# Dilated attention in blocks of one parity: seventeen blocks for eighteen, and transposes two blocks at a time

## The chip, the core and the metric

The kernel runs on one core of one Trainium2 chip. A core has five engines with queues of their own: TensorE (PE) multiplies matrices, VectorE (DVE), ScalarE (ACT) and GpSimd (POOL) work on elements, and SyncE (SP) here issues transfers (DMA). SBUF is the working memory with 128 partitions; PSUM, in eight banks, takes TensorE's results. A product has 128 columns of weights, loaded first, and a moving operand of up to 512 columns. The metric is the time of one execution on the device in microseconds, and less is better.

## The reference

A layer of 2048 tokens with 448 features, in bf16: attention, then a gated mixer, both behind a layernorm and with a residual sum.

```python
def _A_ref(x, wqkv, wo):            # H = 16 heads of Dh = 28
    W, dil = (8, 2)
    qkv = ...x @ wqkv...
    off = jnp.arange(W) * dil
    idx = pos[:, None] - off[None, :]
    mask = idx >= 0
    ...
    logits = jnp.einsum('bhsd,bhswd->bhsw', q, kg) * scale
    attn = _softmax(jnp.where(mask, logits, -1e9), axis=-1)
    o = jnp.einsum('bhsw,bhswd->bhsd', attn, vg)
    return ...o... @ wo

def _B_ref(x, w_in, w_sp, b_sp, w_out):
    z = _gelu(x @ w_in)                      # 448 -> 1792
    z1, z2 = z[..., :896], _layernorm(z[..., 896:])
    g = einsum('ts,bsf->btf', w_sp, z2) + b_sp
    return (z1 * g) @ w_out

h  = x + _A_ref(_layernorm(x), A_wqkv, A_wo)
h2 = h + _B_ref(_layernorm(h), B_w_in, B_w_sp, B_b_sp, B_w_out)
```

A token attends to itself and to the tokens 2, 4, ..., 14 before it, so an even token sees even tokens alone, and an odd one odd tokens alone.

## The kernel before

**Order of work.** The kernel is written as 963 jobs. A job is a few instructions for one engine, with the buffers it reads and writes (`Res`), PSUM banks that it takes or frees (`Ticket`), and an estimate of its time. A planner (`Planner.order`, L273) sorts them in the build: it places one job after another on its engine, by rank from the list `PRIO` among those ready within `LOOK[engine]`, with fixed costs for switching between forms of products (`SWITCH`). What comes out is a fixed order for each engine, and each instruction waits for semaphores of those it depends on. `ON` (L68) puts single jobs on another engine than their usual one.

**Stages.** Tokens lie in 16 tiles of 128. The input tiles get their layernorm (`ln_stats`, `ln_rstd` on POOL, `ln_norm` L682), are transposed to `xhT` (features by tokens; four tiles by TensorE, twelve by DMA), and are projected to queries and keys (`qk`, evacuated by `qe` into `qkT`, [128, 8, 2048], in the order of tokens) in six pieces of tokens (`QT`, L81).

**Attention blocks.** `GEOM` (L17) lists 18 blocks as (first token, queries, keys before it): one of 128 queries, nine of 112 with 16 keys before them, eight of 114 with 14. For each block b:
- `v` (L778): values of the block's 128 keys, two blocks in one job: `xhT` as weights, `wv` moving, evacuated by `ve` into `V1`
- `lg` (L853): 16 products of 28 rows, keys by queries, one for each head, in two jobs; `ex` (L861) exponentiates them from PSUM into `E`, 8 heads at a time
- `mk` (L867): one multiplication by `maskb`, which holds ones on the eight diagonals with a step of two
- `o` (L876): 16 products, `E` as weights, `V1` moving with a column of ones for the sum; `rc` and `om` (L884, L887) normalize into `otm`; `od` copies the last 64 features once more behind the 448, so that after the transpose they lie in both halves of the partitions
- `oT` (L896 to L903): a DMA transpose to `OT` (features by tokens). Where the block's first token isn't a multiple of 16, it goes to a buffer `OTs`, and `oc` copies it on.

As soon as 256 tokens are complete, `project` (L805) multiplies them with `wo` (`y`), adds the residual (`h`, L820), normalizes (`n1`), and transposes each tile by DMA to `hnT` (`hT`, L829).

**Mixer.** `z2` (L912) and `z1` (L960) multiply `hnT` with `w_in`. Eleven of the 16 z2 tiles (`RAW2`) are moved out raw and get their gelu later; the other gelus wait for the last exponential, as ACT loads another table for them. From L1005 on come 28 groups of 16 products with the spatial weights (`wsp_la`, `wsp_lb`, `wsp_hi`, loaded by transposing DMAs), the gate (L1023, L1026), and the output product (L1038).

All DMAs are issued by SP in one queue. A product over 448 features is three products of 128 rows and one of 64; in pairs, the two half-height ones use the upper and lower half of the array at the same time (`product`, L552).

Of the kernel before, what the change touches and what calls it, by code (L numbers as in the profile page):

```python
# [5 lines left out]
S_TOK = 2048  # L6
D = 448
# [7 lines left out]
NAB = 18  # L15
OTR = 1024
GEOM = [(0, 128, 0)] + [(128 + 112 * i, 112, 16) for i in range(9)] + [(1136 + 114 * i, 114, 14) for i in range(8)]  # L17
# [7 lines left out]
LOOK = {'pe': 0.009410205530073946, 'act': 1e-09, 'dve': 0.19498114580727732, 'pool': 1e-09, 'sp': 0.13408016923274957}  # L25
PRIO = [0, 2, 3, 4, 1, 5, 9, 10, 8, 6, 7, 11, 13, 14, 12, 22, 23, 38, 39, 34, 44, 47, 49, 0, 0, 19, 16, 12, 9, 13, 29,
# [36 lines left out]
KEY = dict(x=-10.145, xs=0.685, qk=-3.702, qkg=-1.064, v=-1.761, ve=-6.148, qe=-3.15, lg=-1.488, ex=5.497,  # L63
           mk=-3.215, o=2.696, om=0.603, oT=-1.054, hh=0.0, y=-5.759, h=0.564, ln2=4.478, hT=19.942, z2=74.834,
           z2s=0.028, zr=2.556, zrs=0.21, z1=34.42, z1s=2.041, g=84.462, gs=0.172, wo=1.509, wl=-9.273,
           wls=4.361, wp=-9.955)
WINB = 2
ON = {'xe0_1': 'act', 'nd0_10': 'dve', 'nd0_12': 'dve', 'nd0_13': 'dve', 'nd0_14': 'dve', 'nd0_15': 'dve', 'wp0_1':  # L68
      'act', 'wp1_1': 'act', 'wp2_0': 'act', 'wp2_1': 'act', 'wp3_1': 'act', 'qe4_1': 'dve', 'qe4_3': 'dve', 'nd1_0': 'dve',
      'od3': 'dve', 'od4': 'dve', 'nd1_3': 'dve', 've8': 'dve', 'od9': 'dve', 'nd1_8': 'dve', 'oc12': 'act', 'nd1_10': 'dve',  # L70
      'od14': 'dve', 'oc15': 'act', 'nd1_13': 'dve', 'nd1_14': 'dve', 'nd1_15': 'dve', 'z2c2': 'dve', 'z2c4': 'dve', 'z2c7':
# [1039 lines left out]
```

## Time and profile before

| what | value |
|---|---|
| median of 3 runs | 243.84 us (242.87 to 244.76) |
| the profiled execution | 242.9 us, span of its profile 241.2 us |
| granted TensorE clock | 1.00 |
| DMA | 23.23 MB in 66,468 packets, 46.1% of 16 engines' span in the queue for loads and transposes |
| first spatial product (L1014) | starts at 111.1 us |
| last logit product, last weighted sum | start at 79.3 and 98.0 us |
| transposes issued by SP | 12 to xhT, 11 to OT, 7 to OTs, 16 to hnT, 32 of spatial weights |

The profile page gives each engine's busy time, the span in 40 slices, and the chain of work that ended last. Rows of groups name a line, an engine and an operation, out<-in tiles, shapes, and how often (x): total busy time and the mean of one. Matrix products overlap, so the duration of one (354 ns for 448 columns) is longer than the distance from one to the next; the distance is read from the chain or the timeline. "L565" is the line of a helper that issues all products over 448 features, and "L576" that of a helper for copies, so tile names tell them apart. DVE and ACT in slices of 6 us, in tenths of busy time:

| engine | page, 40 slices |
|---|---|
| DVE | 4799778989989999999761344024044724410754 |
| ACT | 2899868777885899555030000000000000302100 |
| POOL | 7335300233454212431401000000000000000000 |

### The profile page before, as it was taken

To read this page: it belongs to the slowest core of one execution; us is meant where nothing else is said; L and a number is where in the kernel's file an instruction comes from. 1 tells how busy PE (TensorE), PEld (TensorE's weight loads), DVE (VectorE), ACT (ScalarE), POOL (GpSimd) and SP (SyncE) were. 2 spreads that over 40 slices of the span, in tenths; PEclk is the share of its full clock that TensorE was granted. 3 is DMA by queue.
4 is the path that set the end of the run, shared out by engine and by line. 5 is a ranking of instruction groups with operands and counts; after the bars stand their busy time and mean duration, and the time that the engine had idled before them with its cause. 6 is when DMAs were issued, how large, how long until landed. Compare 5 with 4: busy or idle time off the path is not lost.

```text
span 241.2 us, 4323 instructions
## 1 busy us (share of the span) xinstructions
PE 234.0 (97%) x1736; PEld 114.3 (47%) x1758; DVE 152.7 (63%) x330; ACT 93.6 (39%) x118; POOL 42.4 (18%) x93
## 2 busy tenths in 40 slices
PE   7899999999999999999999999999999999999995
PEld 5665445454545444544444444444444544444443
DVE  4799778989989999999761344024044724410754
ACT  2899868777885899555030000000000000302100
POOL 7335300233454212431401000000000000000000
PEclk9999999999999999999999999999999999999999
DMA  6936475975955957967599960000000111000012
GB/s 188 347 98 91 100 148 108 161 214 106 96 117 97 154 102 161 111 136 215 109 188 168 193 127 3 0 0 0 0 3 1 57 38 41 19 0 0 19 60 76
DMA packets 66468, 23.23 MB, mean 96 GB/s; under 512 B 58896, under 2 KB 66192, under 8 KB 66448
## 3 DMA queue, kind: packets, MB, share of 16 engines
q1 hardware_dynamic: 66448, 22.95, 46.1%
q8 instruction: 14, 0.23, 0.4%
q14 instruction: 6, 0.05, 0.1%
HBM read 6.83 MB, written 1.84 MB: 36 GB/s over the span
## 4 chain that ended last, share of the span: by engine, by line
PE 80%; DVE 10%; POOL 3%; DMA 2%; issue 1%; SPq 1%; ACT 1%; DVEq 0%
PE psum L1014 40%; PE psum L565 27%; PE psum L1038 9%; DVE E L867 3%; DMA x_tm<-in_A_x_dram 2%; PE psum L876 2%; DVE st L677 2%; DVE xn L688 2%; POOL rs L672 2%; PE psum L852 2%; SPq L591 1%; DVE otm L887 1%; POOL rs L671 1%; DVE x_tm L820 1%; ACT E L861 1%
## 5 line engine op out<-in xcount | busy, mean ns | idle before, releaser
L1014 PE MATMUL psum<-wsp_hi,z2p 128*128 128x512 bf16 x217 | 50.9, 379 | 0.5 <-issue 0.2
L981 ACT ACTIVATE z1p<-psum 128x1024 bf16<-128x1024 f32 x14 | 14.1, 1024 | 94.3 <-PE psum L565 94.3
L1023 DVE TENSOR_TENSOR ub<-psum,bb 128x512 bf16<-128x512 f32 x28 | 19.4, 692 | 45.3 <-PE psum L1014 44.8
L861 ACT ACTIVATE E<-psum 128x896 bf16<-128x896 f32 (+2 forms) x36 | 31.7, 929 | 8.4 <-PE psum L852 8.4
L1014 PEld LDWEIGHTS psum<-wsp_hi,z2p 128*128 128x128 bf16 x224 | 21.8, 98 | 26.4 <-issue 0.4
L565 PE MATMUL psum<-xhT,wqk 128*128 128x512 bf16 (+5 forms) x185 | 27.8, 306 | 1.6 <-DVE wqk L576 0.8
L1014 PE MATMUL psum<-wsp_lb,z2p 128*128 128x512 bf16 x111 | 26.3, 379 | 0.1
L1014 PE MATMUL psum<-wsp_la,z2p 128*128 128x512 bf16 x109 | 25.7, 379 | 0.2
L565 PE MATMUL psum<-w_in,hnT 128*128 128x448 bf16 (+1 forms) x128 | 25.0, 353 | 0.0
L565 PE MATMUL psum<-hnT,w_in 128*128 128x512 bf16 (+1 forms) x108 | 23.4, 379 | 0.3 <-issue 0.2
L1038 PE MATMUL psum<-w_out,z1p 128*128 128x448 bf16 (+1 forms) x119 | 22.5, 341 | 0.0
L867 DVE TENSOR_TENSOR E<-E,maskb 128x1792 bf16<-128x1792 bf16 (+2 forms) x18 | 19.5, 1098 | 1.1 <-ACT E L861 1.0
L940 DVE BATCH_NORM_STATS2 st<-z2p 128x6 f32<-128x448 bf16 x32 | 18.9, 610 | 1.9 <-ACT z2p L936 1.7
L677 DVE BATCH_NORM_STATS2 st<-x_tm 128x6 f32<-128x448 bf16 x32 | 19.1, 612 | 1.3 <-DMA x_tm<-in_A_x_dram 0.9
L1026 DVE TENSOR_TENSOR z1p<-ub,z1p 128x512 bf16<-128x512 bf16 x28 | 11.8, 424 | 12.4 <-ACT z1p L981 11.6
L565 PEld LDWEIGHTS psum<-xhT,wqk 128*128 128x128 bf16 (+1 forms) x192 | 12.9, 97 | 12.4 <-issue 2.9
L672 POOL TENSOR_TENSOR rs<-rs,negh 128x2 f32<-128x2 f32 (+2 forms) x22 | 17.8, 810 | 1.8
L1045 DVE TENSOR_TENSOR srg<-psum,x_tm 128x448 bf16<-128x448 f32 (+1 forms) x17 | 10.0, 595 | 11.4 <-PE psum L1038 11.2
L1014 PEld LDWEIGHTS psum<-wsp_lb,z2p 128*128 128x128 bf16 x112 | 10.9, 98 | 13.2 <-issue 0.2
L1014 PEld LDWEIGHTS psum<-wsp_la,z2p 128*128 128x128 bf16 x112 | 10.9, 98 | 13.1 <-issue 0.2
L1038 PEld LDWEIGHTS psum<-w_out,z1p 128*128 128x128 bf16 x119 | 11.6, 98 | 10.2
L576 ACT ACTIVATE qkT<-psum 128x1024 bf16<-128x1024 f32 (+2 forms) x22 | 15.4, 716 | 2.5 <-PE psum L565 1.9
(57 smaller groups left out, 229.1 us busy)
## 6 DMA issues: line engine op xcount, KB each, us to landing
w_in<-in_B_w_in_dram SPq DMA_DIRECT2D x8, 224.0 KB, 3.4
out_dram<-srg SPq DMA_DIRECT2D x16, 112.0 KB, 1.7
x_tm<-in_A_x_dram SPq DMA_DIRECT2D x3, 448.0 KB, 6.7
w_out<-in_B_w_out_dram SPq DMA_DIRECT2D x1, 784.0 KB, 6.7
wraw<-in_A_wqkv_dram SPq DMA_DIRECT2D x1, 672.0 KB, 5.7
bb<-in_B_b_sp_dram SPq DMA_DIRECT2D x1, 512.0 KB, 4.7
wv<-in_A_wqkv_dram SPq DMA_DIRECT2D x1, 336.0 KB, 6.7
wo<-in_A_wo_dram SPq DMA_DIRECT2D x1, 336.0 KB, 6.1
```

The costliest lines, as they stand in the source:

```text
L565: ins = e.matmul(o, w, x, start=g not in seen, stop=left[g] == 0, **kw)
L576: j = pl.job(name, eng, key, [(lambda e: e.activation(o(), i(), AF.Copy) if eng == "act" else e.tensor_copy(o(), i()), list(reads), list(w ...
L672: (lambda e: e.tensor_tensor(R, A, negh[:, 0:1].to_broadcast([128, n]), ALU.pow), [rr, r_negh], r_rs[k][m:m + n])],
L677: [(lambda e: e.bn_stats(st[:, m, :], src), [rsrc], [r_st[k][m]])], dve_t(D))
L861: return e.activation(o, i, AF.Exp, scale=SCALE)
L867: return e.tensor_tensor(a, a, maskb[:, 0:1, pad:pad + nq].to_broadcast([NK, NHEAD, nq]), ALU.mult)
L940: [(lambda e, m=m, k=k: e.bn_stats(st3[:, m, k, :], z2p[:, m, D * k:D * (k + 1)]), [r_z2[m]], [r_st[2][m]])], dve_t(D))
L981: return e.activation(o, i, AF.Gelu_apprx_tanh)
L1014: ins = e.matmul(psv(tk), z2p[:, s, 128 * fc:128 * fc + 128], w[:, 512 * (tc % 2):512 * (tc % 2) + 512], start=(s == 0), stop=(s == NB - 1))
L1023: [(lambda e, tc=tc, s=s, tk=tk: e.tensor_tensor(ub[:, s, :], psv(tk), bb[:, 512 * tc:512 * tc + 512], ALU.add), [r_bb], [r_ub[s]])], dve_ ...
L1026: [(lambda e, fc=fc, tc=tc, s=s: e.tensor_tensor(z1p[:, fc, 512 * tc:512 * tc + 512], ub[:, s, :], z1p[:, fc, 512 * tc:512 * tc + 512], AL ...
L1038: ins = e.matmul(psv(tk, 0, c1 - c0), z1p[:, fc, 128 * m:128 * m + 128], w_out[:, fc, c0:c1], start=(fc == 0), stop=(fc == FC7 - 1))
```

## The change

Blocks are now of one parity. `GEOM` holds (first token, queries, keys before it, step): blocks 0 and 1 take the 128 even and the 128 odd tokens of the first 256; then seven pairs take 240 tokens each, 120 queries with 8 keys before them; the last block, 112 queries with 16 keys before it, has step one again. That makes 17. In a block of one parity the mask is a band of eight diagonals in a row, so `maskb` has two masks, one for either kind.

What follows from it:
- `qkT` holds even tokens first, then odd ones, 1024 apart; `qe` writes them apart as it leaves PSUM. For the last block, the last 128 tokens are also copied to `qkL` in order.
- `values` reads every second token of `xhT` as weights.
- Two blocks of a pair lie side by side in `otm` (four slots, before three) and are transposed in one DMA to `OTs`, then `oc` copies both into every second column of `OT`, in two pieces where the ring of 1024 tokens wraps. Eight such copies, on ACT by default; `ON` puts five of them on POOL. The last block is transposed straight to `OT`.
- The second layernorm's tiles are transposed two at a time; `hnT` is now [128, tile, 4, 128], and the reads of `z2` and `z1` follow.
- `bb` (the spatial bias) moves to the place of the attention buffers, and `pads` clears more columns of `E`.
- `PRIO`, `LOOK` and `ON` are new; `KEY`, `RAW2`, `WLH`, `QT` and the stages' code behind attention are the same but for the layout.

```diff
-NAB = 18
+NAB = 17
-GEOM = [(0, 128, 0)] + [(128 + 112 * i, 112, 16) for i in range(9)] + [(1136 + 114 * i, 114, 14) for i in range(8)]
+GEOM = [(r, 128, 0, 2) for r in range(2)] + [(256 + 240 * i + r, 120, 8, 2) for i in range(7) for r in range(2)] + [(1936, 112, 16, 1)]
-LOOK = {'pe': 0.009410205530073946, 'act': 1e-09, 'dve': 0.19498114580727732, 'pool': 1e-09, 'sp': 0.13408016923274957}
...
+LOOK = {'pe': 1e-09, 'act': 0.13510754282655793, 'dve': 0.16074023548447497, 'pool': 0.11561503826604316, 'sp':
+        0.32411456716513315}
...
-ON = {'xe0_1': 'act', 'nd0_10': 'dve', 'nd0_12': 'dve', 'nd0_13': 'dve', 'nd0_14': 'dve', 'nd0_15': 'dve', 'wp0_1':
-      'act', 'wp1_1': 'act', 'wp2_0': 'act', 'wp2_1': 'act', 'wp3_1': 'act', 'qe4_1': 'dve', 'qe4_3': 'dve', 'nd1_0': 'dve',
-      'od3': 'dve', 'od4': 'dve', 'nd1_3': 'dve', 've8': 'dve', 'od9': 'dve', 'nd1_8': 'dve', 'oc12': 'act', 'nd1_10': 'dve',
-      'od14': 'dve', 'oc15': 'act', 'nd1_13': 'dve', 'nd1_14': 'dve', 'nd1_15': 'dve', 'z2c2': 'dve', 'z2c4': 'dve', 'z2c7':
-      'dve', 'z2c10': 'dve'}
+ON = {'xe0_1': 'act', 'nd0_9': 'dve', 'wp0_1': 'act', 'wp1_0': 'act', 'wp1_1': 'act', 'wp2_0': 'act', 'wp2_1': 'act',
+      'wp3_0': 'act', 'qe4_1': 'dve', 'qe4_3': 'dve', 'oc1': 'pool', 'nd1_1': 'dve', 've2': 'dve', 'od2': 'dve', 'oc3':
+      'pool', 'od4': 'dve', 'oc5': 'pool', 'oc7': 'pool', 've8': 'dve', 'od8': 'dve', 'od9': 'dve', 'nd1_6': 'dve', 've10':
+      'dve', 'od13': 'dve', 'oc13': 'pool', 'nd1_12': 'dve', 'nd1_13': 'dve', 'nd1_15': 'dve'}
...
-        hnT = sb("hnT", [128, 4, S_TOK], BF16)
+        hnT = sb("hnT", [128, NB, 4, 128], BF16)
...
+        def qkv(c, lo, hi):
+            return qkT[:, c, :].rearrange("p k (r t) -> p k t r", r=2)[:, :, lo // 2:hi // 2, :]
...
-        pool("pads", -58, [(lambda e: e.memset(E[:, :, NHEAD * 112:NHEAD * 114 + 14], 0.0), [], r_E)], 0.3)
+        pool("pads", -58, [(lambda e: e.memset(E[:, :, NHEAD * 112:ESL], 0.0), [], r_E)], 0.6)
...
+                qops = [(lambda e, eng, lo=lo, hi=hi, g=g, n=n, tk=tk: copy(e, eng, qkv(slice(2 * g, 2 * g + 2), lo, hi), psk(tk, 0, n).rearrange(
+                    "p k (t r) -> p k t r", r=2)), [r_qk[t][g]])]
+                if hi == S_TOK:
+                    qops.append((lambda e, eng, g=g, n=n, tk=tk: copy(e, eng, qkL[:, 2 * g:2 * g + 2, :], psk(tk, n - 128, n)), [r_qkL[g]]))
...
-                    [(i, psv(tk, i, D), xhT[:, c, k0:k0 + NK], wv[:, c, :], None) for i, k0 in enumerate(k0s) for c in range(3)],
+                    [(i, psv(tk, i, D), xhT[:, c, k0:k0 + sd * NK - sd + 1:sd], wv[:, c, :], None) for i, k0 in enumerate(k0s) for c in range(3)],
...
-            for i in range(2):
-                s = ln_norm(1, m + i, mv2, x_tm, r_h[m + i], kl, True)
-                ht_jobs.append(dma_T("hT%d" % (m + i), lambda m=m + i: hnT[:, :, 128 * m:128 * m + 128], lambda s=s: xn[:, s, :],
-                      [r_xn[s], r_xnd[s]], [r_hn[m + i]], kt))
+            ss = [ln_norm(1, m + i, mv2, x_tm, r_h[m + i], kl, True) for i in range(2)]
+            ht_jobs.append(dma_T("hT%d" % m, lambda m=m: hnT[:, m:m + 2].rearrange("p s c t -> p (s c) t"),
+                                 lambda s=ss[0]: xn[:, s:s + 2, :], [r_xn[s] for s in ss] + [r_xnd[s] for s in ss], r_hn[m:m + 2], kt, two=True))
...
+                if b % 2:
+                    ps = b // 2 % 2
+                    dma_T("oT%d" % b, lambda ps=ps: OTs[:, ps].rearrange("p r c t -> p (r c) t"), lambda os=os: otm[:, os - 1:os + 1, :],
+                          r_otm[os - 1:os + 1] + r_otd[os - 1:os + 1], [r_OTs[ps]], b + KEY["oT"], two=True)
+                    cops, a = [], 0
+                    while a < nq:
+                        o = (t0 - 1 + 2 * a) % OTR
+                        n = min(nq - a, (OTR - o) // 2)
+                        cops.append((lambda e, eng, a=a, o=o, n=n, ps=ps: copy(
+                            e, eng, OT[:, :, o:o + 2 * n].rearrange("p c (t r) -> p r c t", r=2), OTs[:, ps, :, :, a:a + n]),
+                            [r_OTs[ps]], [q for rr in r_OT[o // 16:(o + 2 * n) // 16] for q in rr]))
+                        a += n
+                    moves("oc%d" % b, "act", b + KEY["oT"], cops, {"act": act_t(8 * nq), "pool": 1.6})
...
-                    [(i, psv(tk, i), w_in[:, c, 128 * fc:128 * fc + 128], hnT[:, c, 512 * tc:512 * tc + 512], None)
+                    [(i, psv(tk, i).rearrange("p (m t) -> p m t", m=4), w_in[:, c, 128 * fc:128 * fc + 128], hnT[:, 4 * tc:4 * tc + 4, c, :], None)
```

`copy` issues the activation or the tensor copy, by engine; `moves` is `move` for a job of several such copies; `psk` is a stretch of two PSUM banks.

More of the change, by code (lines that the diff above doesn't have):

```diff
@@ L502, in bass_sequential_preLN__sliding_local_dilated__mixer_gmlp__prompt_kernel @@
         r_V = [spot("V%d" % i, o_v + i * NHEAD * 64, NHEAD * 64) for i in range(NV)]
-        r_OT = [spot("OT%d" % i, o_ot, 4 * (OTR + 16) * 2, gen=1) for i in range(OTR // 2 + 8)]
+        r_OT = [[spot("OT%d_%d" % (i, k), o_ot, 4 * OTR * 2, gen=1) for k in range(2)] for i in range(OTR // 16)]
         r_OTs = [Res("OTs%d" % i) for i in range(2)]
@@ L517, in bass_sequential_preLN__sliding_local_dilated__mixer_gmlp__prompt_kernel @@
         r_win2 = Res("w_in2")
-        r_bb = Res("bb")
+        r_bb = spot("bb", o_bb, 2 * S_TOK, gen=2)
         r_ident = Res("ident")
-        r_mask = Res("mask")
+        r_mask = [Res("mask%d" % i) for i in range(2)]
+        r_qkL = [Res("qkL%d" % g) for g in range(4)]
         r_warm = spot("warm", o_warm, 1024)
@@ L579, in move, with copy, moves, psk @@
             return j
+        def copy(e, eng, o, i):
+            return e.activation(o, i, AF.Copy) if eng == "act" else e.tensor_copy(o, i)
+        def moves(name, eng, key, ops, durs, use=(), rel=None):
+            eng = ON.get(name, eng)
+            j = pl.job(name, eng, key, [(lambda e, f=f: f(e, eng), list(rr), list(ww)) for f, rr, ww in ops], durs[eng], use=use, rel=rel)
+            j.alts = durs
+            return j
+        def psk(tk, a, b):
+            return psum[:, tk.b * 512:tk.b * 512 + 1024].rearrange("p (k t) -> p k t", k=2)[:, :, a:b]
+        def qkv(c, lo, hi):
+            return qkT[:, c, :].rearrange("p k (r t) -> p k t r", r=2)[:, :, lo // 2:hi // 2, :]
         def evac_t(n):
@@ L693, in ln_norm, with dma_T @@
             return s
-        def dma_T(name, dst, src, reads, writes, key):
-            return load(name, dst, src, writes, 1.3, (TLAT, 0.95), key=key, transpose=True, reads=reads)
+        def dma_T(name, dst, src, reads, writes, key, two=False):
+            return load(name, dst, src, writes, 1.4 if two else 1.3, (0.95, 1.35) if two else (TLAT, 0.95), key=key, transpose=True,
+                        reads=reads)
         def kx(m):
@@ L768, in bass_sequential_preLN__sliding_local_dilated__mixer_gmlp__prompt_kernel @@
                 product("qk%d_%d" % (t, g), key, f, r_pad[2 * g:2 * g + 2] + xh_res(lo, hi), n, 6, tk, hreads=r_pad2 + xh_res(lo, hi))
-                move("qe%d_%d" % (t, g), "act", lo / 112.0 + KEY["qe"] + KEY["qkg"] * g,
-                     lambda lo=lo, hi=hi, g=g: qkT[:, 2 * g:2 * g + 2, lo:hi],
-                     lambda n=n, tk=tk: psum[:, tk.b * 512:tk.b * 512 + 1024].rearrange("p (k t) -> p k t", k=2)[:, :, 0:n],
-                     [], [r_qk[t][g]], evac_t(2 * n), [tk], tk)
+                qops = [(lambda e, eng, lo=lo, hi=hi, g=g, n=n, tk=tk: copy(e, eng, qkv(slice(2 * g, 2 * g + 2), lo, hi), psk(tk, 0, n).rearrange(
+                    "p k (t r) -> p k t r", r=2)), [r_qk[t][g]])]
+                if hi == S_TOK:
+                    qops.append((lambda e, eng, g=g, n=n, tk=tk: copy(e, eng, qkL[:, 2 * g:2 * g + 2, :], psk(tk, n - 128, n)), [r_qkL[g]]))
+                moves("qe%d_%d" % (t, g), "act", lo / 112.0 + KEY["qe"] + KEY["qkg"] * g, [(f, [], w) for f, w in qops],
+                      {e: sum(evac_t(q)[e] for q in [2 * n, 256][:len(qops)]) for e in ("act", "dve")}, [tk], tk)
         o_jobs = {}
@@ L806, in project @@
             lo, hi = 128 * m, 128 * m + 256
-            blast = [b for b, g in enumerate(GEOM) if g[0] + g[1] >= hi][0]
+            blast = [b for b, g in enumerate(GEOM) if (b % 2 or g[3] == 1) and g[0] + g[3] * (g[1] - 1) + 1 >= hi][0]
             key = blast + KEY["y"]
             kh, kl, kt = blast + KEY["h"], blast + KEY["ln2"], blast + KEY["hT"]
-            rot = [r_OT[(t % OTR) // 2] for t in range(lo, hi, 2)]
+            rot = [q for t in range(lo, hi, 16) for q in r_OT[(t % OTR) // 16]]
             tk = Ticket(2)
@@ L837, in bass_sequential_preLN__sliding_local_dilated__mixer_gmlp__prompt_kernel @@
                 values(b)
-            t0, nq, pad = GEOM[b]
+            t0, nq, pad, sd = GEOM[b]
             slot = b % NE
@@ L841, in bass_sequential_preLN__sliding_local_dilated__mixer_gmlp__prompt_kernel, with f @@
             for t, (lo, hi) in enumerate(QT):
-                if lo < t0 + nq and hi > t0 - pad:
-                    rq += r_qk[t]
+                if lo < t0 + sd * nq and hi > t0 - sd * pad:
+                    rq += r_qk[t] if sd == 2 else r_qkL
             for j in range(2):
                 tk = Ticket(2)
-                def f(e, t0=t0, nq=nq, k0=t0 - pad, j=j, tk=tk):
+                def f(e, nq=nq, pad=pad, q0=t0 % 2 * 1024 + t0 // 2 if sd == 2 else pad, src=qkT if sd == 2 else qkL, j=j, tk=tk):
                     for g in range(4):
@@ L851, in f @@
                             c = (tk.b + i) * 512 + 128 * g
-                            ins = e.matmul(psum[:, c:c + nq], qkT[p:p + DH, 2 * g + 1, k0:k0 + NK],
-                                           qkT[p:p + DH, 2 * g, t0:t0 + nq], start=True, stop=True,
+                            ins = e.matmul(psum[:, c:c + nq], src[p:p + DH, 2 * g + 1, q0 - pad:q0 - pad + NK],
+                                           src[p:p + DH, 2 * g, q0:q0 + nq], start=True, stop=True,
                                            tile_position=(p, 0))
@@ L964, in f @@
                 return (
[L965 removed]
+                    [(i, psv(tk, i).rearrange("p (m t) -> p m t", m=4), w_in[:, c, 128 * fc:128 * fc + 128], hnT[:, 4 * tc:4 * tc + 4, c, :], None)
                      for i, (fc, tc) in enumerate(pair) for c in range(3)],
[L967 to L968 removed]
+                    [(i, psv(tk, i).rearrange("p (m t) -> p m t", m=4), w_in[64 * i:64 * i + 64, 3, 128 * fc:128 * fc + 128],
+                      hnT[64 * i:64 * i + 64, 4 * tc:4 * tc + 4, 3, :], (64 * i, 0)) for i, (fc, tc) in enumerate(pair)])
             rh = []
@@ L989, in bass_sequential_preLN__sliding_local_dilated__mixer_gmlp__prompt_kernel @@
              after=[o_jobs[NAB - 1]])
-        wl_ev = [o_jobs[min(b, NAB - 1)] for b in range(19)] + ht_jobs
-        late = ht_jobs[NB - 1]
+        wl_ev = [o_jobs[min(b, NAB - 1)] for b in range(19)] + [h for h in ht_jobs for _ in range(2)]
+        late = ht_jobs[-1]
         for s in range(NB):
```

64 lines of the change are left out of this document (31 added, 33 removed), and 71 rows, old and new, of the table PRIO.

## The prediction

> **What bounds the kernel now.** I read the page's first, second and fourth part, then the waits of TensorE alone, the windows of four stages, and the rows of the chain of waits for prices. From the page, TensorE's share of the span and the chain by engine:
>
> ```profile
> PE 234.0 (97%) x1736; PEld 114.3 (47%) x1758; DVE 152.7 (63%) x330; ACT 93.6 (39%) x118; POOL 42.4 (18%) x93
> ...
> PE 80%; DVE 10%; POOL 3%; DMA 2%; issue 1%; SPq 1%; ACT 1%; DVEq 0%
> ```
>
> A busy TensorE need not be a full one, so the next view is what it waits for (total us, times, longest):
>
> ```profile
> PE psum L1053 <- DVE warm L646: 1.5, 1, 1.5
> PE psum L565 <- DVE wqk L576: 0.8, 1, 0.8
> PE psum L565 <- issue: 0.6, 4, 0.2
> PE psum L852 <- DVE x_tm L820: 0.3, 1, 0.3
> ```
>
> The first two lie before 9 us. After that one wait of 0.3 us on another engine is all: the matrix products run one behind the other from 13 us to the end. In the windows the columns are the stage, its length, and busy time of PE, weight loads, DVE, ACT, POOL:
>
> ```profile
> 0.00:12.00 12.00, 9.66 (x98) 7.01 (x98) 7.65 (x23) 6.46 (x16) 6.62 (x25) 1.00 0.86 267
> 12.00:60.00 48.00, 47.16 (x589) 24.18 (x594) 42.56 (x95) 39.00 (x48) 13.31 (x26) 1.00 0.62 127
> 60.00:111.00 51.00, 50.52 (x451) 24.24 (x456) 48.57 (x110) 40.16 (x47) 17.49 (x32) 1.00 0.73 128
> 111.00:241.00 130.00, 126.66 (x604) 58.84 (x613) 53.97 (x107) 7.97 (x9) 4.95 (x10) 1.00 0.27 57
> ```
>
> From 12 to 111 us, where all of the change lies, DVE is busy 91.1 of 99 us and ACT 79.2: both follow close behind TensorE, and at 62 to 74 us the chain does run through DVE. But first-layer products of the mixer stand ready and fill TensorE there, so DVE costs nothing yet. The clock is 1.00 throughout. So a change pays here by TensorE's own time, or it costs by making TensorE wait.
>
> **TensorE's part of the change.** Prices come from the chain (start, us, what):
>
> ```profile
> 51.61 0.54 PE psum L565 x4
> ...
> 59.65 0.33 PE psum L852 x16
> ...
> 61.22 0.80 PE psum L876 x32
> ...
> 200.21 1.32 PE psum L1038 x7
> ```
>
> One attention block fewer removes its 16 logit products, 0.33 us (row L852), and its 16 weighted sums, 0.80/2 = 0.40 us (row L876). The value projection goes from nine pairs of blocks to eight pairs and a single: three full products fewer, at 1.32/7 = 0.189 us for 448 columns, 0.57 us. The two half-height products of a pair run side by side, and the single one takes as long as a pair, so nothing is saved there. A change from one form of product to another costs about 0.1 us: four half-height products of 512 columns are two side-by-side pairs, 2 x 0.189 x 512/448 = 0.43 us, and the first row above takes 0.54. A block brings about two such changes: 0.2 us (0 to 0.4). Sum: 0.33 + 0.40 + 0.57 + 0.20 = 1.5 us less.
>
> Nothing is added to it: the blocks have 120 queries in place of 112 or 114, but 16 logit products take 0.33 us in rows with 112 as in rows with 114, and before 14 us, with 128, the next product starts 0.33 us behind the first too. The value products now load every second token as weights. A weight load lasts 97 ns behind a product of 189 ns, so one of twice the length (194 ns) would show 5 ns on each of 51 full loads: 0 to 0.3 us, taken as 0, since no row loads with a step. The mixer's first products read their moving tokens in four pieces of 128 in place of one run of 512; as the pieces are still runs, I take 0.
>
> **The other engines' part, off the path.** ACT: an exponential of 960 columns, between 917 ns (896) and 1028 (1024), is 0.973 us. Now 4 x 1.028 + 28 x 0.973 + 2 x 0.917 = 33.2 us replace 32.1: +1.1. The table of engines gives three value moves to DVE and makes the last one half as long: -2.3. Four z2 moves come back to ACT: 4 x 0.922 = +3.7. The last query tile is moved once more for the single block, 4 x 0.383 = +1.5. Three attention copies of 960 columns (0.593 us for 456, 0.87 ns a column: 1.03) replace two of 0.593: +2.0 with one split in two. One weight move: +0.5. Together +6.5, 85.7 of the same 99 us. DVE: -4.3 (z2), +2.2 (values), -1.3 (copies), -0.9 (one normalization by the row sums), -1.2 (small copies and weights), -0.1 (masks): -5.6, 85.5 of 99. Both stay under TensorE; without that cover each us above 99 would be paid in full.
>
> POOL gets five attention copies of 960 columns. Its rows are a 64-column copy at 0.24 us when not held up, and a memset of 512 columns at 0.52: 1 to 2 us each, 5 to 10 us in an engine busy 31 of 99. Behind each in POOL's queue stand reciprocal roots of the layernorms (0.38 + 0.76 us), which DVE waits for. The copy that ACT keeps waits for its transpose, and behind it stand exponentials of later blocks; two of the seven copies stood so before. I take 0 for these waits, up to 1 us.
>
> SP: 34 transposes (18 of attention output, 16 of the second layernorm) at 1.21 us of issue each become 9 and 8. A pair is as wide as the spatial weight's transposes, 1.30 us to issue and 3.4 to 4.1 to land, where a single one landed in 2.5. SP's queue gets some 41 - 22 = 19 us shorter between 25 and 124 us, so w_in and spatial-weight loads behind them leave earlier; the pair lands 1 to 1.6 us later and its first half waits for its second. What then comes late is the output projection of 256 tokens. TensorE has other products meanwhile: 0, up to 1 us.
>
> **Rivals.**
>
> A, the forecast: the block's 1.5 us comes off and nothing else shows. The profiled run of before took 242.9 us (span 241.2), so 241.4; against the median of the three runs, 243.84, it is 242.3. Own range 241.1 to 243.3. Chance 0.50.
>
> B, more than that: the order of all work is new. Half-height products stand in some 29 groups of the timeline at about 0.2 us a group for entering and leaving, and the first 12 us hold 27 warming products (5.7 us) and the 2.3 us of waits. Ten groups merged, or a start earlier by 1 to 2 us, give 1 to 2.5 more: 239.8 to 241.3. Against it: the loads and the first layernorm set that start, and they stay. Chance 0.22.
>
> C, slower: the copy that moves queries and keys out of PSUM now writes even and odd tokens to two places 2 KB apart, element by element. These 22 copies hold 15.4 us of ACT, of which 10 x 1024 + 4 x 512 + 8 x 256 = 14,336 columns at 0.87 ns are 12.4. They lie between 9 and 60 us, where ACT has 48 - 39 = 9 us free. So a factor up to 1.7 per column is hidden, and at twice the time 12.4 + 1.5 (more exponentials and one copy) - 9 = 5 us are paid by TensorE, which never gets them back: 243.8 - 1.5 + 5 = 247.3 (246 to 249). No row steps so. Memsets in pieces of four columns, one piece in each 64 bytes, ran at 0.82 ns a column (from 0.20 us for 128 columns to 0.52 for 512), as runs do: against it. One of single columns, 64 bytes apart, took 0.52 us for 96, though beside a DVE memset that ended with it: for it. ACT writes pieces of 28 at full rate (923 ns for 896). Chance 0.17.
>
> The Trainium skill (SBUF — State Buffer, the note on cachelines under Door 1: The DMA port swizzle) says that SBUF has lines of 16 bytes and that at least two accesses in a row must hit one line to run at full speed; by that rule every write of this copy leaves its line, the rule speaks against the change, and the time would be C's. The same note counts steps of up to 8 bf16 elements as free, by which the attention copies, stepping two, would not pay.
>
> D, the block's time is given back: pairs arrive in bursts, TensorE waits for a projection or a logit tile where the order had none before, 1 to 2 us in all: 243.3 to 245.3. For it: one such wait (0.3 us at 74 us) exists, and the copies and transposes are longer links. Against it: the fill of mixer products. Chance 0.11.
>
> **The numbers.** About 1% (2.4 us) is what a measurement of this kernel tells from no change; its three runs lie 1.9 us apart. Faster by over 1%, below 241.4: all of B and some 0.08 of A, 0.30. Slower by over 1%, above 246.3: most of C, 0.17. Within: 0.53. The time is A's, 242.3. For 8 in 10 the range goes from 240.0 (B's far end left out, 0.07) to 247.2 (C's upper half, 0.09).
>
> **What would show it.** In the changed profile: 272 logit and 272 weighted-sum products in place of 288; a logit row of 16 still at 0.33 us; TensorE's waits after 13 us still under 1 us, and the spatial product starting near 109 to 110 us where it starts at 111.1 now (A). An earlier first logit or fewer half-height groups: B. A qkT copy of 1024 columns far over 1.03 us, with logits waiting for ACT: C. Waits of TensorE on the copies to OT, or on DVE's residual sum: D. A V weight load far over 190 ns, or POOL copies of over 3 us with DVE waiting for the roots, would make me wrong in a way not listed.

## The result, and the profile after

The changed kernel takes 306.4 us (median of 6 runs, 302.2 to 307.6) against 243.8 for the one before, a ratio of 1.251 [1.242, 1.260]. Its profiled execution took 306.35 us, with a span of 304.6. The forecast was 242.3. Of the rivals, C went the right way, with 247.3.

From the page of the changed kernel: busy time by engine, three rows of the 40 slices (7.6 us each), and the chain by engine.

```profile
PE 259.3 (85%) x1709; PEld 121.4 (40%) x1727; DVE 159.2 (52%) x314; ACT 148.4 (49%) x125; POOL 48.3 (16%) x105
...
PE   7676565758758637999999999999999999999996
...
ACT  3998789955686799698995732000000000004010
...
PEclk9979685565598797599999999999999999999999
...
PE 66%; ACT 24%; DVE 5%; DMA 2%; issue 1%; SPq 1%; POOL 1%; DVEq 0%
```

ACT was 1% of the chain and is now 24%. TensorE is no longer full in the first 16 slices (some 122 us), and its granted clock falls to 0.5 to 0.8 in many of them: where it starves, its products also run longer (a value product lasts 516 ns on average, before 354). From then on the rows look as before. The waits of TensorE (us in total, times, longest) say whom it starves for:

```profile
PE psum L875 <- ACT qkT L582: 13.7, 5, 5.2
PE psum L565 <- ACT qkT L582: 9.5, 7, 2.8
PE psum L565 <- ACT qkL L582: 5.2, 2, 3.0
PE psum L875 <- ACT qkL L582: 5.2, 2, 3.3
PE psum L875 <- DVE qkT L582: 3.3, 2, 2.0
```

Before, one wait of 0.3 us was all that stood behind the start. Three rows name the copy that moves queries and keys out of PSUM, on ACT or on DVE, and two the small copy `qkL` that stands behind it in ACT's queue. In the chain (start, us, what) the copies stand as links of their own, TensorE between them:

```profile
24.93 9.22 ACT qkT L582 x4
...
34.20 0.61 PE psum L875 x13
34.81 2.84 PE psum L565 x7
...
40.95 4.69 ACT qkT L582
```

The copies by shape (count, busy us, mean ns of one), of the changed kernel:

```profile
L582 ACT ACTIVATE qkT<-psum 128x1024 bf16<-128x1024 f32 x10 | 46.9, 4740 | 3.8 <-PE psum L565 3.8
L582 ACT ACTIVATE qkT<-psum 128x256 bf16<-128x256 f32 x8 | 9.4, 1543 | 0.3 <-PE psum L565 0.3
L582 ACT ACTIVATE qkT<-psum 128x512 bf16<-128x512 f32 x4 | 9.2, 2682 | 1.4 <-PE psum L565 1.4
L582 DVE CAST qkT<-psum 128x1024 bf16<-128x1024 f32 x2 | 9.2, 4790 | 5.2 <-PE psum L565 5.2
```

and the two rows of 1024 columns in the kernel before:

```profile
L576 ACT ACTIVATE qkT<-psum 128x1024 bf16<-128x1024 f32 x10 | 10.2, 1026 | 2.1 <-PE psum L565 1.9
L576 DVE CAST qkT<-psum 128x1024 bf16<-128x1024 f32 x2 | 2.5, 1225 | 0.6 <-PE psum L565 0.6
```

So the copy takes 4.6 times as long on ACT and 3.9 times on DVE, for the same columns and types. ACT's 22 copies went from 15.4 to 65.5 us. In windows (length; busy PE, weight loads, DVE, ACT, POOL; clock) the two stages that had TensorE full at clock 1.00 now read:

```profile
12.00:60.00 48.00, 30.06 (x263) 14.32 (x264) 19.65 (x51) 43.22 (x28) 10.27 (x22) 0.75 0.28 63
60.00:111.00 51.00, 34.96 (x309) 15.23 (x312) 29.05 (x37) 35.78 (x23) 7.80 (x11) 0.73 0.42 72
```

ACT is busy 43 of 48 us with 28 instructions, where it had 39.0 us for 48. The first spatial product starts at 171.9 us in place of 111.1.

### The profile page after: what moved, and what is told of

It reads as the page before. It is cut to its first block, busy times and chain, and to the rows that moved or that the text cites. A ratio compares the mean times of both kernels' runs of the same rounds, so it can differ in the third digit from the quotient of the medians.

```text
span 304.6 us, 4231 instructions
## 1 busy us (share of the span) xinstructions
PE 259.3 (85%) x1709; PEld 121.4 (40%) x1727; DVE 159.2 (52%) x314; ACT 148.4 (49%) x125; POOL 48.3 (16%) x105
## 4 chain that ended last, share of the span: by engine, by line
PE 66%; ACT 24%; DVE 5%; DMA 2%; issue 1%; SPq 1%; POOL 1%; DVEq 0%
PE psum L1044 32%; PE psum L565 24%; ACT qkT L582 21%; PE psum L1068 7%; DVE qkT L582 3%; PE psum L875 3%; ACT E L884 2%; DMA wraw<-in_A_wqkv_dram 2%; PE psum L899 1%; SPq L606 1%; DVE xn L708 0%; DVE st L697 0%; DVE x_tm L844 0%; POOL rs L691 0%; ACT qkL L582 0%
## 5 line engine op out<-in xcount | busy, mean ns | idle before, releaser
L582 ACT ACTIVATE qkT<-psum 128x1024 bf16<-128x1024 f32 (+2 forms) x22 | 65.5, 3203 | 5.5 <-PE psum L565 5.5
L565 PE MATMUL psum<-xhT,wqk 128*128 128x512 bf16 (+5 forms) x186 | 36.2, 361 | 12.8 <-ACT qkT L582 8.1
L884 ACT ACTIVATE E<-psum 128x960 bf16<-128x960 f32 (+2 forms) x34 | 32.5, 998 | 16.3 <-PE psum L875 16.3
L890 DVE TENSOR_TENSOR E<-E,maskb 128x1920 bf16<-128x1920 bf16 (+2 forms) x17 | 19.8, 1167 | 22.8 <-ACT E L884 22.8
L875 PE MATMUL psum<-qkT 28*128 28x120 bf16 (+1 forms) x256 | 12.6, 255 | 22.1 <-ACT qkT L582 13.7
L565 PE MATMUL psum<-wv,xhT 128*128 128x448 bf16 (+1 forms) x68 | 22.4, 516 | 4.5 <-ACT qkL L582 3.0
L565 PEld LDWEIGHTS psum<-xhT,wqk 128*128 128x128 bf16 (+1 forms) x192 | 14.4, 105 | 28.9 <-issue 10.4
L875 PEld LDWEIGHTS psum<-qkT 28*128 28x128 bf16 x256 | 7.7, 109 | 31.7 <-ACT qkT L582 12.0
L691 POOL TENSOR_SCALAR rs<-mv 128x2 f32<-128x2 f32 (+2 forms) x22 | 8.7, 395 | 61.6 <-DVE mv L699 46.7
L692 POOL TENSOR_TENSOR rs<-rs,negh 128x2 f32<-128x2 f32 (+2 forms) x22 | 16.8, 765 | 1.8
```

The lines of the kernel that those rows point to most:

```text
L565: ins = e.matmul(o, w, x, start=g not in seen, stop=left[g] == 0, **kw)
L582: return e.activation(o, i, AF.Copy) if eng == "act" else e.tensor_copy(o, i)
L692: (lambda e: e.tensor_tensor(R, A, negh[:, 0:1].to_broadcast([128, n]), ALU.pow), [rr, r_negh], r_rs[k][m:m + n])],
L875: ins = e.matmul(psum[:, c:c + nq], src[p:p + DH, 2 * g + 1, q0 - pad:q0 - pad + NK], src[p:p + DH, 2 * g, q0:q0 + nq], start=True, stop=True,
L884: return e.activation(o, i, AF.Exp, scale=SCALE)
L890: return e.tensor_tensor(a, a, maskb[:, mi:mi + 1, pad:pad + nq].to_broadcast([NK, NHEAD, nq]), ALU.mult)
```

## Experiments

Theory: the slow copy, element by element to two places, makes the whole loss. Rivals: something else in the change makes a good part of it (the pairs and their transposes, POOL's copies, the new order), or the copy is slow for another reason than its writes. Later runs ask where the forecast's 1.5 us went.

**The changed kernel with the copy in runs.** The same elements go to the same places, but all even tokens of a piece first, then all odd ones. The write is two runs, and PSUM is read in steps of two.

```diff
-            return qkT[:, c, :].rearrange("p k (r t) -> p k t r", r=2)[:, :, lo // 2:hi // 2, :]
+            return qkT[:, c, :].rearrange("p k (r t) -> p k r t", r=2)[:, :, :, lo // 2:hi // 2]
...
-                    "p k (t r) -> p k t r", r=2)), [r_qk[t][g]])]
+                    "p k (t r) -> p k r t", r=2)), [r_qk[t][g]])]
```

> The changed kernel; only the copy of queries and keys out of PSUM goes through the same elements in another order: all even tokens of a tile, then all odd ones, so that it reads PSUM in steps of two and writes in runs. Theory (the write pattern alone makes the change slow): the copies of 1024 columns take 1.0 to 2.1 us in place of 4.74, the granted clock is 1.00, and the time is 242 us (241 to 244) if steps of two in PSUM are read at full rate, 245 to 250 if at half rate. Rival (pairs of blocks and longer links starve TensorE): the copies are as fast, but the time stays above 255 us.

Measured: 244.6 us (244.1 to 245.7), ratio to before 1.0047 [1.0018, 1.0076]. Of the 62.6 us, 61.8 are gone. The copies by shape, and the chain by engine, of this kernel:

```profile
L582 ACT ACTIVATE qkT<-psum 128x1024 bf16<-128x1024 f32 x10 | 10.3, 1028 | 2.6 <-PE psum L565 2.6
...
L582 DVE CAST qkT<-psum 128x1024 bf16<-128x1024 f32 x2 | 2.5, 1226 | 0.8 <-PE psum L565 0.8
```

```profile
PE 71%; DVE 16%; DMA 5%; POOL 4%; issue 2%; ACT 0%; POOLq 0%; DVEq 0%
```

The prices of before are back, though PSUM is now read in steps of two, so reading isn't what costs. The clock is 1.0 again. But the kernel is not faster than before: by the medians of these runs it is 1.0 us slower (244.6 against 243.6), where the forecast had 1.5 less and the theory above 242.

**The changed kernel with queries and keys in token order.** `qe` writes as before, and the logit products take every second token, both as weights and as moving operand.

```diff
-                            ins = e.matmul(psum[:, c:c + nq], src[p:p + DH, 2 * g + 1, q0 - pad:q0 - pad + NK],
-                                           src[p:p + DH, 2 * g, q0:q0 + nq], start=True, stop=True,
+                            ins = e.matmul(psum[:, c:c + nq], qkT[p:p + DH, 2 * g + 1, k0:k0 + sd * (NK - 1) + 1:sd],
+                                           qkT[p:p + DH, 2 * g, q0:q0 + sd * (nq - 1) + 1:sd], start=True, stop=True,
...
```

> The changed kernel with queries and keys kept in the order of tokens, as before the change: the copy reads and writes in runs, and the logit products take every second token as weights and as moving operand; the second copy for the last block falls away. Theory: copies of 1024 columns at 1.03 us, 16 logit products at 0.33 to 0.40 us, time 241 to 243 us. Rival (pairs of blocks starve TensorE): above 255 us. Should steps of two slow the logit products, 16 of them take over 0.5 us and the time is 243 to 247.

Measured: 247.3 us, 1.0149 [1.0104, 1.0194]. The loss is gone here too, by the other way round. A logit product of 120 columns takes 214 ns with steps of two, and 213 without. The theory's 241 to 243 us is missed, and most of the 2.7 us against the run above isn't the steps': 1.9 of them lie ahead of the first logit product, which comes at 15.63 us in place of 13.76 behind the same products. These run slower there: nine warming products take 2.10 us in place of 1.16, and twelve first projections 1.49 in place of 0.83, though the clock column reads 1.00. The last 0.8 us were not traced; without the copies to `qkL` the order also differs a little.

**The kernel before with the alternating copy alone.** Nothing else of the change; attention then reads other tokens' queries and keys.

```diff
-                     lambda lo=lo, hi=hi, g=g: qkT[:, 2 * g:2 * g + 2, lo:hi],
-                     lambda n=n, tk=tk: psum[:, tk.b * 512:tk.b * 512 + 1024].rearrange("p (k t) -> p k t", k=2)[:, :, 0:n],
+                     lambda lo=lo, hi=hi, g=g: qkT[:, 2 * g:2 * g + 2, lo:hi].rearrange("p k (r t) -> p k t r", r=2),
+                     lambda n=n, tk=tk: psum[...].rearrange("p (k t) -> p k t", k=2)[:, :, 0:n].rearrange("p k (t r) -> p k t r", r=2),
```

> The kernel before with one thing of the change: the copy of queries and keys writes even and odd tokens of a tile to two places, element by element (half a tile apart); the attention then reads keys of other tokens than the reference's. Theory: copies of 1024 columns near 4.7 us, granted clock near 0.9, time 295 to 310 us. Rival (the blocks and their order make the loss, the copy a part of it): copies as slow, but a time under 275 us.

Measured: 298.1 us, 1.2239 [1.2195, 1.2284], so 54.5 us more than before, from one access pattern. Its ACT copies of 1024 columns have a mean of 4.84 us, DVE's 4.78, the granted clock is 0.914. Taking the pattern out of the changed kernel (61.8 us) and putting it alone into the old one (54.5) agree up to 7 us, which were not traced.

**The copy by itself.** A kernel of nothing but copies of 1024 columns, three of each kind, first on DVE, then on ACT, each waiting for the one before.

> Copies by themselves, 1024 columns on 128 partitions, DVE first, then ACT, each pattern three times; the layer is left out and the output is zeros. Theory (a write that leaves the 16 bytes of the one before it costs some 4.6 ns, on either engine): alternating columns 4.7 us at either distance, steps of 8 and 16 columns 4.7 us as well, steps of two at most 1.3 us, runs of two columns about 2.4 us, runs of eight 1.1 us; reading PSUM in steps of two 1.0 to 2.1 us. Rival (any write of two bytes that is not in a run is slow): steps of two and four as slow as alternating. Rival (the jump of 2 KB is what costs): distance 1024 slower than 544, and steps of 16 fast.

Rows of groups (busy us, mean ns of one). From PSUM: L40 contiguous, L43, L46, L49 and L52 writing every second, fourth, eighth and sixteenth place, L55 alternating between two places 2 KB apart, L61 the same in runs of two, L70 reading PSUM in steps of two. From SBUF: L79, alternating.

```profile
L49 ACT ACTIVATE buf<-psum 128x1024 bf16<-128x1024 f32 x3 | 14.1, 4692 | 0.1
...
L55 ACT ACTIVATE buf<-psum 128x1024 bf16<-128x1024 f32 x3 | 14.0, 4678 | 0.1
...
L55 DVE CAST dvb<-psum 128x1024 bf16<-128x1024 f32 x3 | 14.0, 4666 | 0.1
...
L52 ACT ACTIVATE buf<-psum 128x1024 bf16<-128x1024 f32 x3 | 13.3, 4437 | 0.1
...
L79 DVE COPY dvb<-src 128x1024 bf16<-128x1024 bf16 x3 | 8.2, 2744 | 0.1
L46 ACT ACTIVATE buf<-psum 128x1024 bf16<-128x1024 f32 x3 | 7.3, 2432 | 0.1
...
L43 ACT ACTIVATE buf<-psum 128x1024 bf16<-128x1024 f32 x3 | 3.9, 1302 | 0.1
...
L61 ACT ACTIVATE buf<-psum 128x1024 bf16<-128x1024 f32 x3 | 3.1, 1050 | 0.1
L40 ACT ACTIVATE buf<-psum 128x1024 bf16<-128x1024 f32 x3 | 3.1, 1023 | 99.4 <-DVE dvb L79 99.3
...
L70 ACT ACTIVATE buf<-psum 128x1024 bf16<-128x1024 f32 x3 | 3.1, 1023 | 0.1
```

What follows: it is the write. From PSUM, a two-byte write whose neighbour is not the next one written costs up to 4.6 ns, the same on ACT and DVE, which differ by 20% on runs (1023 and 1224). From SBUF it is not: DVE's alternating copy (L79) takes 2.7 ns a column, ACT's 4.6 (4710 ns). From PSUM the price grows with the step (1.27, 2.4, 4.6 ns a column at steps of two, four, eight), and the distance of the two places doesn't matter: 1088 bytes (L58, 4678) cost as 2 KB. Runs of two, which jump half as often, cost nothing, where the theory had expected half the price. One rule, an estimate from these rows, fits all of them from PSUM roughly: lone two-byte writes pay 4.3 to 5.1 ns for each new 16 bytes that they enter (5.1, 4.8, 4.6 and 4.3 at steps of two, four, eight and sixteen), and a pair pays nothing. It doesn't fit DVE's copy from SBUF, and it was not tested further.

The Trainium skill (SBUF — State Buffer, the note on cachelines under Door 1: The DMA port swizzle) has lines of 16 bytes, of which at least two accesses in a row must hit the same for full speed. The alternating copy agrees in direction, and the note gives no price. It also counts up to 8 bf16 elements as a free step; here writes stepping four already take 2.4 times as long and stepping two 1.3 times, so for ACT's and DVE's writes the measurement decides.

**A shorter memset.** The forecast's 1.5 us is still missing, and the start is one suspect: `pads` now clears 1024 columns, and DVE's first normalization stands beside it. In the timeline (start, us) of the changed kernel with the copy in runs, against 0.40 us for the same normalization before:

```profile
4.74 1.67 DVE L708 TENSOR_SCALAR xn<-x_tm,mv,rs 128x448 bf16<-128x448 bf16 x1 [1.02 <-POOL rs L692]
4.91 0.52 POOL L669 MEMSET V<- 128x96 bf16 x1
5.03 1.25 POOL L666 MEMSET E<- 128x1024 bf16 x1
...
6.46 0.34 PE L739 MATMUL psum<-ident,xn 128*128 128x128 bf16 x3 [0.93 <-DVE xn L708]
```

The normalization ends 0.13 us after the memset of `E`, and TensorE waits 0.93 us for it. Only 16 columns need clearing:

```diff
-        pool("pads", -58, [(lambda e: e.memset(E[:, :, NHEAD * 112:ESL], 0.0), [], r_E)], 0.6)
+        pool("pads", -58, [(lambda e: e.memset(E[:, 2:4, NHEAD * 120:NHEAD * 120 + 8], 0.0), [], r_E)], 0.6)
```

> As e1_runs, and the clearing of E's columns on POOL is cut from 1024 columns to 16 (the eight columns behind 1920 in two of the four buffers, which the first weighted sums there read; all other columns are written before they are read). In e1_runs that memset lasts from 5.03 to 6.28 us, and DVE's first normalization, 0.40 us before the change, lasts from 4.74 to 6.41. Theory (the two hold the same port, so the first tile of the layernorm comes 1.1 to 1.3 us late, TensorE waits 0.9 us and its clock may come up late): the normalization takes 0.40 us, the first transposing product starts near 5.3 us, the first logit product 0.5 to 1.2 us earlier, and the time falls by 0.5 to 1.5 us against e1_runs, to about 243.5. Rival (the start is set by loads and by the second tile): the normalization is short, and the time stays within 0.3 us of e1_runs.

Measured: 244.2 us (12 runs, 243.6 to 245.7), 1.0039 [1.0015, 1.0063]. The normalization takes 0.93 us, not the expected 0.40: POOL's memset of `V` (0.52 us) still stands beside it. The first transposing product starts at 5.71 us in place of 6.46, but the first logit product comes at 13.55 in place of 13.76, as TensorE now waits 0.39 us for a later normalization. The time is the same within the intervals. This memset is not where the 1.5 us went.

**Logit jobs on alternate halves.** The two logit jobs of a block use the lower and the upper half of the array's rows. In the order of the changed kernel many neighbours are of the same half. From the timeline of the kernel with the copy in runs:

```profile
24.71 0.41 PE L875 MATMUL psum<-qkT 28*128 28x120 bf16 x16
...
32.96 0.59 PE L875 MATMUL psum<-qkT 28*128 28x120 bf16 x16
33.49 0.61 PE L565 MATMUL psum<-xhT,wqk 64*128 64x512 bf16 x4
```

The next row starts 0.53 us behind the second of these 16 products, and 0.34 behind the first. Here five blocks exchange their two jobs, in the same order of the jobs:

```diff
-            for j in range(2):
+            for jj in range(2):
+                j = jj ^ (b in (4, 7, 10, 11, 14))
...
```

> As e1_runs, and five blocks (4, 7, 10, 11, 14) exchange the names of their two logit jobs, so that the same places of the order now hold the other half of their heads. In e1_runs 16 logit products take 0.52 us where both jobs use the same rows of the array (heads of the same half, seven times), and 0.33 to 0.35 where they use different rows. Theory (products on different rows run side by side): all rows of 16 take 0.33 to 0.36 us, logit products in all 1.2 to 1.4 us less, and the time falls by as much, to about 243.3 us. Rival (0.52 us comes from 120 columns a product in place of 112): no row changes, the time stays.

Measured: 245.3 us (11 runs, 243.9 to 246.1), 1.0064 [1.0036, 1.0092]. Of eight rows with both jobs on one half (the expectation counted seven) seven are cured, as the same place of the timeline shows:

```profile
32.95 0.41 PE L876 MATMUL psum<-qkT 28*128 28x120 bf16 x16
```

All logit rows together, each from its start to the next row's, take 8.1 us in place of 9.35. The time does not follow: its interval overlaps that of the copy in runs, and its median lies above. Inconclusive: 1.3 us on TensorE's own timeline are either given back elsewhere or lost in the spread of 2 us.

**Both together.** The two edits above in one kernel.

> e5 and e6 together. Theory: the two gains add, 1.7 to 2.9 us below e1_runs, 241.7 to 242.9 us, that is 0.3 to 0.8% below the kernel before: what one block fewer was to bring (1.5 us) is there once the copy, the memset and the halves no longer cost. Rival (one block fewer is worth nothing on this order): the time stays at that of the kernel before or above.

Measured: 244.4 us (243.1 to 246.4), 1.0058 [1.0029, 1.0087]. No sum of two gains is seen. The profiled execution, the longest of the twelve, shows one source of the spread: DVE's first copy of weights comes at 7.85 us, after 2.1 us of waiting for their load, where the kernel with the short memset alone has it at 5.57, and the first logit product comes at 15.10 us in place of 13.55. So the landing of the first loads alone moves the start by as much as the change was to save.

**What a block's products are worth in a given order.** If TensorE has slack, removing products doesn't pay in full. Here products are added instead: the logit products and weighted sums of six blocks are issued twice, the second over the first, in the kernel before and in the changed one with the copy in runs and the short memset. No order changes.

```diff
-                    for g in range(4):
+                    for g in (0, 1, 2, 3) * (2 if b in (4, 6, 8, 10, 12, 14) else 1):
...
```

> The kernel before, its order unchanged, with the logit products and the weighted sums of six blocks (4, 6, 8, 10, 12, 14) issued twice, the second over the first: what TensorE pays for six blocks' products when nothing else moves. Theory (TensorE's own time is paid in full in a given order): a block's weighted sums 0.40 us, its logits 0.33, or 0.52 as the second pass of a job stands on the same half of the array; six times 0.73 to 0.92, so 4.4 to 5.5 us more, 248.0 to 249.1 us against 243.6. Rival (the order has slack in which products vanish): under 3 us more, and then the forecast's saving would never have been full, whatever the order.

> The same doubling of six blocks in the change with the copy in runs and 16 cleared columns (244.18 us): theory, 4.4 to 5.5 us more, 248.6 to 249.7 us; rival, under 3 us more. If the kernel before pays in full and this one does not, the new order has idle time on TensorE that the old one lacks.

Measured: before, doubled, 248.7 us, 1.0188 [1.0136, 1.0241], so 4.6 us more (3.3 to 5.9). On TensorE's timeline logits went from 7.1 to 9.0 us and weighted sums from 9.1 to 11.9: 4.7 us, all of which the time shows. The changed one, doubled: 248.6 us, 1.0190 [1.0146, 1.0233] to before; against the 1.0039 without doubling that is some 3.7 us more (2.5 to 4.9, an estimate from the two intervals), 4.4 by medians, with 4.3 on the timeline. For the kernel before the theory holds: in its order each added product is paid in full, 0.77 us a block, near the forecast's 0.73. For the changed one the timeline agrees, but the time alone doesn't rule out the rival's 3 us. Removing products in a given order was not run.

**The order chosen anew.** That leaves the order itself. The kernel with both edits got ranks from three searches of some 26,000 small random changes each, kept where the planner's own plan became shorter. The plan counted 0.2 us more for two neighbouring logit jobs on the same half, and 0.1 in place of 0.6 us for the short memset. All three plans are 1.2 us shorter.

> The change with the copy in runs, 16 cleared columns and exchanged halves (244.41 us), and now with the ranks chosen anew: 26,000 small random changes of the ranks, kept where the planner's own time came out shorter, with 0.2 us added in its plan for two logit jobs in a row on the same half. Its plan is 1.2 us shorter (238.9 against 240.1 us). Theory (the block's 1.5 us was given back by the order of the work: logit jobs alone or on the same half, changes of form): 242.9 to 243.6 us, and TensorE's stretch from the first logit product to its end drops by about 1 us. Rival (given back in places no order changes, the start of the kernel and the transfers): 244.2 to 245.0 us.

> The same with the ranks of a second search from another seed; its plan is 238.95 us, 1.2 us shorter. Theory (order): 242.9 to 243.6 us. Rival (not the order): 244.2 to 245.0 us. If one of the two searches is faster and the other isn't, the plan's time is no guide at this size.

> The same with the ranks of a third search; its plan is 238.94 us, 1.2 us shorter, and it has no two logit jobs in a row on the same half. Theory (order): 242.9 to 243.6 us. Rival (not the order): 244.2 to 245.0 us.

Measured: 248.2, 247.8 and 251.5 us; ratios 1.0194 [1.0107, 1.0281], 1.0173 [1.0096, 1.0250] and 1.0330 [1.0248, 1.0411]. Neither side expected this: the shorter plans are 3 to 7 us slower on the chip than the same kernel in its old order (1.0058). In the second, TensorE has new waits (us in total, times, longest), this one, 1.2 us for `hnT` and 0.7 for a normalization:

```profile
PE psum L610 <- POOL OT L627: 1.8, 1, 1.8
```

The plan sets a product where it thinks a copy or a transpose just done, and on the chip it isn't. In the other two the waits behind the start are 0.8 to 2.2 us in all, and part of their loss lies at the end. Behind TensorE's last product DVE still has residual sums to make, and there they wait for the store of an earlier one. In the third (start, us):

```profile
245.00 0.62 DVE L1102 TENSOR_TENSOR srg<-psum,x_tm 128x448 bf16<-128x448 f32 x1 [1.78 <-DMA out_dram<-srg]
247.40 0.62 DVE L1102 TENSOR_TENSOR srg<-psum,x_tm 128x448 bf16<-128x448 f32 x1 [1.78 <-DMA out_dram<-srg]
```

There 7.6 us pass from the end of TensorE's last product to the end of the span, in the first of the three 4.4, and 2.7 in the kernel before and in all those with the old order. That is 4.9 of the third's 7 us and 1.7 of the first's 3; the rest wasn't traced. What the three show is that the same work in another order differs by up to 7 us, several times the 1.5 us at stake, and that a plan's own microsecond is no guide at this size. They don't show that no order keeps the 1.5 us. No kernel here beats the one before.

## Why the prediction was wrong

**What failed is the price of the copy.** The forecast A put it at nothing: its sum for ACT (+6.5 us) counts every other move and leaves these 22 as they were. Only rival C gave it a price, and there the mechanism was named: the copy out of PSUM writes even and odd tokens apart, element by element, ACT pays and TensorE never gets it back. The step "at twice the time 12.4 + 1.5 - 9 = 5 us" took a factor of two, for which no row stood; the chip has 4.6, and ACT's 50 us more are over five times what was free, with 6.7 us more on DVE beside them. The row that had the price was quoted there: the memset of single columns 64 bytes apart, 0.52 us for 96. One of a single column takes 0.10, so it is (521 - 98) / 95 = 4.5 ns a column, which is near the 4.3 to 4.6 that the copy by itself measured. I set it aside as slowed by a DVE memset; but in the profiles it lasts 0.51 to 0.52 us beside a DVE normalization too. Taken as it stood, 14,336 columns at 4.5 ns are 64 us in place of 12.4, and 243.8 - 1.5 + 64 - 12.4 + 1.5 - 9 = 286 us. The other row, pieces of four columns at 0.82 ns, consists of runs, and runs of two already cost nothing. The chance of 0.17 and a range ending at 247.2 both rest on that choice: a mechanism with an unknown price needs the far row as its end.

**What the price left out.** From 286 to 306: the copies on DVE, the small copies queued behind on ACT, and TensorE's clock, 0.73 to 0.75 between 12 and 111 us. The forecast let TensorE run at 1.00 while it waits. These were not told apart.

**The forecast's saving.** A fell too: cured of the copy, the kernel stands 0.4 to 0.6% above before, 2.5 to 3 us from where A had it. The doubling doesn't speak against its price of a block: it finds 0.77 us for the logits and sums (0.33 + 0.40 forecast), and the products are 272 and 272 as forecast. Full rows kept their 189 ns with weights in steps of two (weight loads 98 ns, before 97). What failed is the sentence that nothing is added: logits in the new order take longer in all, with one block fewer. TensorE's timeline, each row from its start to the next row's start, in us:

| rows | before | copy in runs, short memset | forecast | measured |
|---|---|---|---|---|
| logit products | 7.11 | 8.83 | -0.3 | +1.7 |
| weighted sums | 9.08 | 7.69 | -0.4 | -1.4 |
| products over 448 features, full height | 78.84 | 79.60 | -0.6 | +0.8 |
| the same, half height | 16.27 | 16.48 | 0 | +0.2 |
| spatial and output products | 117.84 | 118.36 | 0 | +0.5 |

Changes of form, forecast at -0.2, are inside these rows. Logits were taken at 0.33 us a block, but that holds for two halves side by side; the new order puts eight pairs on one half (0.52 to 0.68, before one) and leaves eight jobs alone (0.31 each, before four). The last three rows decide nothing. The same order with the long memset has 78.16 and 17.27 in the third and fourth, and in the doubled kernel before, where these products are as before and no record of them is missing, the third and fifth are 80.03 and 118.28. From the first logit product to the end of TensorE's last one, the kernel before takes 225.3 us and the kernels with the copy in runs and the old order 226.4 to 226.9, where the forecast had 223.8. What else makes this up stays open: curing the halves didn't lower the time, and in the two doubled kernels the new order is 0.5 us the shorter (230.2 against 230.7).

**The rest, step by step,** in the kernel with the copy in runs, for the changed one hides it. Exponentials of 960 columns: 973 ns, as forecast; but their term of +1.1 us was wrong, as it set counts times means (33.2) against a busy time (32.1). Counts times means give 33.4 before, so -0.2. ACT between 12 and 111 us: 82.5 us (forecast 85.7); DVE 88.1 (85.5). POOL's copies to `OT`: 1.5 us each (1 to 2). ACT's: 1.30 (1.03), the step of two being the 1.3 of the copy by itself. Pairs of transposes land in 3.3 us (3.4 to 4.1), 16 of them and one single. TensorE's waits behind the first products: 0.9 us in all (under 1). Spatial products start at 110.6 us (109 to 110). B had no sign: the order had more half-height groups, 31 for 29. D's bursts showed as small waits on `E` and `hnT`, 0.2 to 0.4 us each.

## What to carry to other kernels

When a copy's access pattern changes, price its writes from a row with that same pattern, however odd the row. In copies from PSUM to two-byte elements keep at least two in a row on the writing side and read PSUM in steps of two to reorder: one swapped loop was worth 62 us here. Here a saving of 1.5 us in a full order of 240 us was smaller than what the order itself and the first loads move, so it had to be measured in the new order; the sum of its parts didn't forecast it.

## What the runs showed of the hardware

- In alternating copies of 1024 columns from PSUM, a lone two-byte write to SBUF cost ACT and DVE the same 4.6 ns. From SBUF, DVE's alternating copy took 2.74 us (427 ns contiguous) and ACT's 4.71 (1056).
- A starved TensorE ran at a granted clock of 0.73 to 0.75 on average between 12 and 111 us, though only one core was at work, and at 1.00 in the cured kernel.
- At the start, TensorE's warming products of 256 columns were 213 ns apart and later 109. With the copy in runs the short distance was reached before 7 us, with queries and keys in token order not before 10, and the first logit product came 1.9 us later.
- Sixteen logit products of 28 rows took 0.34 us with the two jobs on different halves of the array's rows and 0.53 with both on one.
- DVE's normalization of 0.40 us took 1.67 beside POOL memsets of 0.52 and 1.25 us, which ran from 4.91 to 6.28 us, and 0.93 beside two that ran from 4.89 to 5.41.
